# Attention with pooled queries and a gated MLP on one core: the remainder of each tile of p in two instructions, a planner that may prefer a form of product, and new ranks

## The chip, the cores and the metric

The kernel runs on one core of a Trainium2 chip. The metric is device time in microseconds (us) of one execution; the times are given as a median over repeated executions. The core has TensorE (PE, matrix products; PEld is its weight load), VectorE (DVE), ScalarE (ACT), GpSimd (POOL) and SyncE (SP, which here only issues transfers).

## The reference, cut to what matters

```python
def _attn_ref(q, k, v):                       # each (4, 8, 1152, 64), float32
    q_pool = q.reshape(B, H, S // 2, 2, D).mean(axis=3)
    scores = scale * np.matmul(q_pool, k.transpose(0, 1, 3, 2))
    scores = scores - np.max(scores, axis=-1, keepdims=True)
    attn = np.exp(scores)
    attn = attn / (np.sum(attn, axis=-1, keepdims=True) + 1e-09)
    return np.matmul(attn, v)

x = attn_out.transpose(0, 2, 1, 3).reshape(2304, 512)
h = x @ w_in                                  # w_in (512, 2048)
g = h * (1.0 / (1.0 + np.exp(-1.702 * h)))
return g @ w_out                              # w_out (2048, 512)
```

## The kernel before

**Attention.** The 32 heads are taken as 16 pairs. A pair has 9 tiles of scores, each 128 query rows by 1152 keys: 4 of head A, 4 of head B and one ("L") that holds the last 64 rows of both. That makes 144 tiles, numbered n. The 36 tiles of the first four pairs work in f32: scores (L629), transposes of p on TensorE (L751, evacuated at L256 or L258), and products with v (L774). The other 108 tiles split each f32 operand into an f16 head and an f16 remainder. For such a tile the steps are: S, six products (L658) into the single score buffer `s` of PSUM; M, the row maximum, which also copies the scores to the tile `p` (L672, DVE) and so frees `s`; B, a small addition to the maximum (L705); E, the exponential in place (L679, ACT); H (`p_hi`), the f16 head of p, written to one half of a tile `hl`; L (`p_lo`), the remainder p minus head, 1152 columns, written to the other half (L713, one instruction on DVE or POOL); T (`p_tr`), one DMA transpose of the whole `hl` (L726, queue of SP) into `pt` or `ptl`; then, once four tiles (or the L tile) are there, 54 products with v (L739). There are three `hl` buffers; H of a tile waits until the transpose that read the buffer three tiles back has landed.

**MLP.** Rows of x come in 9 blocks of 256. Each block has 8 steps j: 24 products h (L957), tanh (L965, ACT), gate (L971, DVE), `moe_hi` (g's f16 head, L256) and `moe_lo` (its remainder, L982, DVE), then 12 products o (L993). The f16 weights are made early in the kernel from the raw loads (L283 to L330). A block can start when all heads of its batch are done.

**The order.** Nothing is scheduled by hand. A planner (class `Plan`) holds every step as a task with an engine, a cost, a rank, predecessors and buffers. It simulates the engines and writes the order out; on the chip each engine runs its instructions in that order. At each step the planner takes, for each engine, the tasks that could start within `wait` of the earliest one, and of these the one of the lowest rank; the engine whose choice starts first goes next. A task with `or_on` may go to either of two engines, to whichever comes to it first. `movable` lists the kinds for which the second engine is allowed. Costs are multiplied by `slack` (for PE it is an added delay of each operand from another engine). The planner never lets a POOL task overlap a DVE task marked `two`. Tasks of TensorE carry a `mode`, the form of their product (0: the default, among them f16 scores of A and B, h, o and all transposes; 3: products with v, the rows of reciprocals, f16 scores of L; 4 and 5: f32 scores); a change of mode is charged `SWITCH`, 0.095 us. Ranks are n plus a constant of the kind; products h and o stand at 1,000,000 plus their sequence number, so attention always goes first and the MLP fills in.

`copy(e, ...)` issues an ACT activation (L256), a DVE copy (L258) or, with a scale, a DVE `tensor_scalar` (L260). `x_hi` and `x_even` write the f16 heads of x; `q_hi`, `k_hi`, `v_hi` and `w_hi` those of q, k, v and the weights.

Of the kernel before, what the change touches and what calls it, by code (L numbers as in the profile page):

```python
# [15 lines left out]
ALU = mybir.AluOpType  # L16
# [7 lines left out]
class Plan:  # L24
# [10 lines left out]
    DMA_IN, DMA_OUT, SWITCH = 0.8, 1.6, 0.095  # L35

    def __init__(self, sizes, wait, slack):
        self.sizes, self.wait, self.slack, self.tasks, self.users, self.takers = sizes, wait, slack, [], {}, {}

    def add(self, name, eng, cost, rank, fn, after=(), take=(), use=(), dma=0.0, or_on=None, two=False, mode=0, tr=False):  # L40
# [20 lines left out]
    def order(self):  # L61
        self.busy = {}
        left = {id(t): len(t["after"]) for t in self.tasks}
        ready = {(id(t), e): 0.0 for t in self.tasks for e in t["on"]}
        heirs = {}
        for t in self.tasks:
            for a in t["after"]:
                heirs.setdefault(a, []).append(t)
        pend = dict(self.users)
        ended = {}  # L70
        taken = {tag: [] for tag in self.sizes}
        free = {e: 0.0 for e in ("PE", "ACT", "DVE", "POOL", "SP")}
        queue = {e: [t for t in self.tasks if e in t["on"] and not left[id(t)]] for e in free}
        dma_free, lock, mode, out = 0.0, 0.0, 0, []

        def start(t, e):
            s = max(free[e], ready[id(t), e])
            if e == "POOL" or e == "DVE" and t["two"]:
                s = max(s, lock)
            more = {}  # L80
            for tag, _ in t["take"]:
                held = taken[tag]
                at = len(held) + more.get(tag, 0) - self.sizes[tag]
                more[tag] = more.get(tag, 0) + 1
                if at >= 0:
                    key = held[at]
                    if pend[key]:
                        return None
                    s = max(s, ended[key] + (self.slack["PE"] if e == "PE" else 0.0))
            return s  # L90

        while len(out) < len(self.tasks):
            best = None
            for e, q in queue.items():
                c = [(s, t) for s, t in ((start(t, e), t) for t in q) if s is not None]
                if not c:
                    continue
                s0 = min(s for s, _ in c) + self.wait.get(e, 0.0)
                s, t = min(((s, t) for s, t in c if s <= s0), key=lambda x: (x[1]["rank"], x[0]))
                if best is None or s < best[0]:  # L100
                    best = (s, t, e)
            assert best is not None, "the buffers taken are not given back"
            s, t, eng = best
            for e in t["on"]:
                queue[e].remove(t)
            cost = t["on"][eng]
            if eng != "PE":
                cost *= self.slack[eng]
            if eng == "PE":
                cost += self.SWITCH * (t["mode"] != mode)  # L110
                mode = t["mode"]
            end = free[eng] = self.run_pe(s, cost) if eng == "PE" else s + cost
            if eng == "POOL" or eng == "DVE" and t["two"]:
                lock = end
            if t["tr"]:
                free[eng] = dma_free = max(end, dma_free + t["dma"])
                end = dma_free + 2.05
            elif t["dma"]:
                dma_free = max(s + self.DMA_IN, dma_free) + t["dma"]
                end = dma_free + self.DMA_OUT  # L120
            out.append((t, eng))
            seen = end + self.HOP[eng]
            for tag, key in t["take"]:
                taken[tag].append(key)
            for key in t["use"]:
                pend[key] -= 1
                ended[key] = max(ended.get(key, 0.0), seen)
            for h in heirs.get(t["name"], ()):
                for e in h["on"]:
                    at = free[e] if e == eng and (e == "PE" or h["name"][0] == t["name"][0]) else seen + (self.slack["PE"] if e == "PE" else 0.0)  # L130
                    ready[id(h), e] = max(ready[id(h), e], at)
                left[id(h)] -= 1
                if not left[id(h)]:
                    for e in h["on"]:
                        queue[e].append(h)
        self.span = max(free.values())
        return out
# [3 lines left out]
def kernel(  # L141
# [27 lines left out]
    B, H, S, D = q.shape  # L169
# [14 lines left out]


    rank = dict(
        w1=1635.4577871165, w1_rate=0.1876384407, w2=1964.3304764093, w2_rate=0.0010521929,
        w1_cut=3141.8757239327, w1_cut_rate=51.5930924503, w2_cut=-186.6998375499, w2_cut_rate=1.8487508169,
        v_max=330.999166611, load=-550.3041412927, prep=894.9078087958, max=-1755.14139546,
        exp=-460.1572995655, p_hi=-10.305124868, p_lo=1244.8028802268, pv=1153.6831869514, x=1717.9360493586,  # L190
        recip=1660.8177940748, w_tr=1074.7852256343, w_ev=329.2480174456, g=-2009.7431374895,
        pv_b=-1699.9111894481, max_b=1557.6887587647, p_lo_b=594.8157896537, prep_b=-1564.592405644,
        v=1630.1595431886, lift=-579.2269003092,
    )
    movable = dict(DVE=('qk_ev', 'w_hi', 'k_hi', 'v_hi', 'x_even', 'w_sign'), POOL=('p_lo', 'denom'))
    wait = dict(PE=0.073718, ACT=0.133022, DVE=0.295657, POOL=0.285145)
    slack = dict(PE=0.297637, ACT=1.031989, DVE=1.023033, POOL=1.19561, SP=1.076504)
    sizes = dict(
        qraw=1, qs=1, kraw=1, kn=1, qn=1, kT=2, qT=2, vraw=2, vhl=1,
        p=3, hl=3, pt=3, ptl=1, xt=2, xf=2, raw=4, th=2, gf=2, g=3, osb=2, s=1, tr=1, pv=1, h=1, o0=1, o1=1,  # L200
    )
    plan = Plan(sizes, wait, slack)
# [32 lines left out]
    T = {}  # L235
# [6 lines left out]
    def on(kind, **cost):  # L242
        return {e: c for e, c in cost.items() if kind in movable[e]}
# [4 lines left out]
    def dve(n, psum=False, fast=False):  # L248
        return n / (1920 if fast else 960) + (0.065 if psum else 0.068)
# [91 lines left out]
    for i in range(32):  # L341
        c, kk = divmod(i, 4)
# [7 lines left out]
            or_on=on("w_exp", POOL=1.06),  # L350
# [10 lines left out]
            take=[("h", cs)] if first else []  # L361
# [8 lines left out]
    for c in range(8):  # L370
        for h in range(2):
            e = 2 * (c % 4) + h
            r = rank["w1_cut"] + e / rank["w1_cut_rate"] if c < 4 else rank["w2_cut"] + e / rank["w2_cut_rate"]
            after = [("w_scale", c // 4)] + [("w_mul", 4 * c + 2 * h + e) for e in range(2)]
            if c:
# [3 lines left out]
                or_on=on("w_hi", DVE=dve(1024, fast=True) + 0.06),  # L379
# [180 lines left out]
    for g in pairs:  # L560
# [7 lines left out]
        for i, (what, a) in enumerate((w, a) for w in "qkv" for a in range(2)):  # L568
            key = (what + "raw", G)
# [3 lines left out]
            if what == "k" and not G:  # L573
# [5 lines left out]
                use=[key] if a else [], dma=1.05,  # L579
# [3 lines left out]
        if g.wide:  # L583
            for i, (what, lo, hi) in enumerate(PARTS):
                pk = ("qkp", G, i)
                take = [(f"o{i % 2}", pk)] + ([("kT", kt)] if i == 0 else [("qT", qt)] if i == 1 else [])
# [121 lines left out]
        t = new("hl", ("hl", n), [128, 2, S], F16)  # L708
        copy(e, t[:, 0, :], T["p", n].rearrange("p c f -> p (c f)"))

    def p_lo(e, n):
        t = T["hl", n]
        (nc.vector if e == "DVE" else nc.gpsimd).tensor_tensor(  # L713
            out=t[:, 1, :], in0=T["p", n].rearrange("p c f -> p (c f)"), in1=t[:, 0, :], op=ALU.subtract
        )

    def p_tr(n):
# [115 lines left out]
    for n, (g, kind, t) in enumerate(tile_of):  # L833
# [25 lines left out]
        if g.whole:  # L859
            for c in range(3):  # L860
                pb = ("pb", n, c)
                plan.add(("X", n, c), "PE", 0.33, n + rank["w_tr"], lambda n=n, c=c: w_tr(n, c),
                         [("E", n)] + ([("X", n, c - 1)] if c else []),
                         take=[(f"o{(3 * n + c) % 2}", pb)], use=[("p", n)])
                plan.add(
                    ("Y", n, c), "ACT", act(384, True), n + rank["w_ev"], lambda e, n=n, c=c: w_ev(e, n, c),
                    [("X", n, c)] + ([("Y", n, 0)] if c else before), take=[] if c else take,
                    use=[pb] + ([key] if c else use), or_on=on("w_ev", DVE=dve(384, True)),
                )
        else:  # L870
            plan.add(("H", n), "ACT", act(1152, ptr=1), n + rank["p_hi"], lambda e, n=n: p_hi(e, n),
                     [("E", n)] + ([("H", n - 1)] if n and not tile_of[n - 1][0].whole else []),
                     use=[("p", n)], take=[("hl", ("hl", n))],
                     or_on=on("p_hi", DVE=dve(1152, fast=True) + 0.06), two=True)
            plan.add(("L", n), "DVE", dve(1152) + 0.06, n + rank["p_lo"] + (rank["p_lo_b"] if n >= 72 else 0.0),
                     lambda e, n=n: p_lo(e, n), [("H", n)], use=[("p", n), ("hl", n)], two=True,
                     or_on=on("p_lo", POOL=2.36))
            plan.add(
                ("T", n), "SP", 2.9, n - 1, lambda n=n: p_tr(n),
                [("L", n)] + before, take=take,  # L880
                use=use + [("hl", n)], dma=1.84, tr=True,
            )
        if kind == "A" or t % 2 == 0 and kind == "B":
# [255 lines left out]
```

## Time and profile before

| what | value |
|---|---|
| median of 3 runs | 800.97 us (798.48 to 801.73) |
| the profiled execution: its own time | 798.88 us |
| the profiled execution: span from first to last instruction | 797.1 us |
| PE busy in it | 767.6 us (96%) |
| ACT, DVE, POOL busy | 601.5 (75%), 564.4 (71%), 270.1 (34%) |

The profile shows one execution. "Busy" is the time in which an engine had at least one instruction; PE's ends are modelled because its products are pipelined. A wait names the instruction that came last before the waiting one could start.

### The profile page before, as it was taken

To read this page: it belongs to the slowest core of one execution; us is meant where nothing else is said; L and a number is where in the kernel's file an instruction comes from. 1 tells how busy PE (TensorE), PEld (TensorE's weight loads), DVE (VectorE), ACT (ScalarE), POOL (GpSimd) and SP (SyncE) were. 2 spreads that over 40 slices of the span, in tenths; PEclk is the share of its full clock that TensorE was granted. 3 is DMA by queue.
4 is the path that set the end of the run, shared out by engine and by line. 5 is a ranking of instruction groups with operands and counts; after the bars stand their busy time and mean duration, and the time that the engine had idled before them with its cause. 6 is when DMAs were issued, how large, how long until landed. Compare 5 with 4: busy or idle time off the path is not lost.

```text
span 797.1 us, 16744 instructions
## 1 busy us (share of the span) xinstructions
PE 767.6 (96%) x6756; PEld 514.8 (65%) x6756; DVE 564.4 (71%) x883; ACT 601.5 (75%) x1031; POOL 270.1 (34%) x164
## 2 busy tenths in 40 slices
PE   6999999999999999999999989999999999999998
PEld 3556565656566676666766666656666667766664
DVE  5867997689988869697787858688867785222222
ACT  5989988899888879697887879787987887232322
POOL 2232222145544442625235354521555423000000
PEclk9999999999999999999999999999999999999999
DMA  8644233459999999999999999999999979010000
GB/s 308 197 154 148 101 120 130 165 117 194 197 193 211 195 204 200 207 214 206 215 192 217 197 202 196 207 194 197 202 222 196 168 130 177 2 27 1 28 1 27
DMA packets 336143, 128.77 MB, mean 162 GB/s; under 512 B 311232, under 2 KB 321472, under 8 KB 336064
## 3 DMA queue, kind: packets, MB, share of 16 engines
q1 hardware_dynamic: 335776, 127.10, 76.7%
q8 instruction: 53, 0.87, 0.4%
q10 hardware_dynamic: 288, 0.59, 0.2%
q14 instruction: 26, 0.21, 0.1%
HBM read 45.09 MB, written 4.72 MB: 62 GB/s over the span
## 4 chain that ended last, share of the span: by engine, by line
PE 59%; DVE 13%; DMA 10%; ACT 7%; issue 6%; POOL 2%; SPq 2%; DVEq 0%; POOLq 0%; ACTq 0%
PE o L993 16%; PE h L957 15%; PE s L658 8%; PE pv L739 8%; DMA pt<-hl 5%; DVE p L672 4%; PE s L629 3%; PE pv L774 3%; PE o L751 3%; DMA ptl<-hl 3%; ACT p L679 2%; ACT hl L256 2%; DMA raw<-in_moe_w_in_dram 2%; PE tr L786 2%; DVE wbuf L330 1%
## 5 line engine op out<-in xcount | busy, mean ns | idle before, releaser
L713 POOL TENSOR_TENSOR hl<-p,hl 128x1152 f16<-128x1152 f32 x75 | 186.3, 2487 | 209.1 <-ACT hl L256 167.5
L672 DVE TENSOR_SCALAR_CACHE_REDUCE p<-s,e_s 128x1152 f32<-128x1152 f32 x144 | 203.5, 1413 | 52.7 <-PE s L658 31.1
L993 PE MATMUL o<-wbuf,g 128*128 128x512 f16 x864 | 206.2, 379 | 0.0
L957 PEld LDWEIGHTS <-wbuf 128*128 128x128 f16 x1728 | 168.0, 98 | 42.7 <-issue 6.8
L679 ACT ACTIVATE p<-p,nm 128x1152 f32<-128x1152 f32 x144 | 180.2, 1251 | 7.7 <-DVE p L672 4.3
L256 ACT ACTIVATE hl<-p 128x1152 f16<-128x1152 f32 x108 | 124.8, 1156 | 25.5 <-DMA pt<-hl 18.7
L993 PEld LDWEIGHTS <-g 128*128 128x128 f16 x864 | 83.0, 98 | 83.8 <-issue 2.3
L658 PE MATMUL s<-kT,qT 128*128 128x384 f16 (+1 forms) x720 | 123.9, 327 | 2.8 <-DVE p L672 2.7
L957 PE MATMUL h<-x16a,wbuf 128*128 128x256 f16 x960 | 118.0, 275 | 1.7 <-DVE gf L971 1.6
L971 DVE SCALAR_TENSOR_TENSOR gf<-th,h 128x512 f32<-128x512 f32 x72 | 49.2, 683 | 81.5 <-ACT th L965 81.3
L965 ACT ACTIVATE th<-h,t_s 128x512 f32<-128x512 f32 x72 | 49.0, 680 | 74.1 <-PE h L957 73.9
L957 PE MATMUL h<-wbuf 128*128 128x256 f16 x768 | 90.9, 273 | 0.7 <-DVE gf L971 0.7
L658 PEld LDWEIGHTS <-qT 128*128 128x128 f16 (+1 forms) x720 | 62.2, 100 | 45.0 <-issue 9.9
L739 PEld LDWEIGHTS <-vhl 128*64 128x64 f16 x1944 | 80.6, 111 | 15.9 <-issue 8.5
L739 PE MATMUL pv<-pt,vhl 128*64 128x256 f16 x1296 | 76.1, 273 | 2.4 <-DMA pt<-hl 2.4
L982 DVE SCALAR_TENSOR_TENSOR g<-gf,g 128x512 f16<-128x512 f32 x72 | 59.0, 819 | 17.3 <-ACT g L256 17.1
L307 POOL TENSOR_TENSOR wbuf<-raw 128x512 f32<-128x512 f32 x32 | 33.7, 1060 | 82.0 <-ACT raw L303 66.8
L256 ACT ACTIVATE g<-gf 128x512 f16<-128x512 f32 x72 | 44.7, 621 | 18.5 <-DVE gf L971 18.5
L713 DVE TENSOR_TENSOR hl<-p,hl 128x1152 f16<-128x1152 f32 x33 | 45.7, 1386 | 12.2 <-ACT hl L256 11.7
L751 PE MATMUL o<-idf,p 128*128 128x128 f32 x324 | 50.1, 284 | 3.5 <-ACT pt L256 2.9
L629 PE MATMUL s<-kT,qT 64*128 64x512 f32 (+3 forms) x240 | 49.5, 524 | 1.5 <-DVE p L672 1.5
L751 PEld LDWEIGHTS o<-idf,p 128*128 128x128 f32 x324 | 35.4, 141 | 19.4 <-ACT pt L256 8.9
(101 smaller groups left out, 790.5 us busy)
## 6 DMA issues: line engine op xcount, KB each, us to landing
vraw<-in_v_dram SPq DMA_DIRECT2D x32, 288.0 KB, 3.5
kraw<-in_k_dram SPq DMA_DIRECT2D x30, 288.0 KB, 4.1
qraw<-in_q_dram SPq DMA_DIRECT2D x32, 256.0 KB, 3.8
raw<-in_moe_w_in_dram SPq DMA_DIRECT2D x16, 512.0 KB, 5.3
raw<-in_moe_w_out_dram SPq DMA_DIRECT2D x16, 512.0 KB, 5.7
out_dram<-osb SPq DMA_DIRECT2D x16, 256.0 KB, 3.0
pt<-hl SPq DMA_TRANSPOSE x96, 5.2
qraw<-in_q_dram SPq DMA_DIRECT2D x32, 32.0 KB, 3.4
```

The costliest lines, as they stand in the source:

```text
L256: nc.scalar.activation(out=out, in_=in_, func=ACTF.Copy, scale=1.0 if scale is None else scale)
L629: nc.tensor.matmul(out=ps[m, bank, 0:128 * (last - first)], lhsT=qT[h, (j - half) % NJ, m], rhs=kT[h, first:last].rearrange("p j c -> p (j ...
L658: nc.tensor.matmul(out=ps[m, c, 0:384], lhsT=st, rhs=T["kT", g.P][:, o:o + 3].rearrange("p r c -> p (r c)"), start=(l == 0), stop=(l == 1),)
L672: nc.vector.tensor_scalar(out=p, in0=s, scalar1=e_s[:, g.P:g.P + 1], scalar2=None, op0=ALU.mult, op1=ALU.min, accum_out=m)
L679: nc.scalar.activation(out=p, in_=p, func=ACTF.Exp, bias=T["nm", n], scale=-1.0, accum_out=sm)
L713: (nc.vector if e == "DVE" else nc.gpsimd).tensor_tensor(out=t[:, 1, :], in0=T["p", n].rearrange("p c f -> p (c f)"), in1=t[:, 0, :], op=A ...
L739: nc.tensor.matmul(out=ps[64 * a:64 * (a + 1), 0:w], lhsT=T["vhl", g.P][:, a, g.block[a][c], m], rhs=pt[:, l * KR + c, o:o + w], start=(pa ...
L751: nc.tensor.transpose(ps[:, 128 * i:128 * (i + 1)], T["p", n][:, c, 128 * i:128 * (i + 1)], idf)
L957: nc.tensor.matmul(out=h[:, e, :], lhsT=w1(2 * j + e, l, kk), rhs=x_rhs(blk, m, kk), start=(kk == 0 and l == 0 and m == 0), stop=(kk == KD ...
L971: nc.vector.scalar_tensor_tensor(out=gf, in0=T["th", blk, j], scalar=1.0, in1=T["h", blk, j].rearrange("p e n -> p (e n)"), op0=ALU.add, o ...
L982: nc.vector.scalar_tensor_tensor(out=g[:, 1].rearrange("p e n -> p (e n)"), in0=T["gf", blk, j], scalar=2.0 ** -16, in1=g[:, 0].rearrange( ...
L993: nc.tensor.matmul(out=o, lhsT=g[:, l, e, 128 * t:128 * (t + 1)], rhs=w2(fc, m), start=(fc == 0 and l == 0 and m == 0), stop=(fc == KFF - ...
```

## The change

`p_lo` becomes two tasks per tile, each of 576 columns, each free to go to DVE or POOL; the transpose waits for both. The planner's choice subtracts `stay` (7.04) from the rank of a PE task whose mode is that of the task before it. `movable` for DVE loses `k_hi`, `v_hi`, `x_even` and gains `x_hi`, `q_hi`, `moe_hi`, `p_hi`. All ranks, the `wait` windows and the `slack` factors are new.

```diff
-                s, t = min(((s, t) for s, t in c if s <= s0), key=lambda x: (x[1]["rank"], x[0]))
+                s, t = min(((s, t) for s, t in c if s <= s0), key=lambda x: (x[1]["rank"] - self.stay * (e == "PE" and x[1]["mode"] == mode), x[0]))
...
-        exp=-460.1572995655, p_hi=-10.305124868, p_lo=1244.8028802268, pv=1153.6831869514, x=1717.9360493586,
-        recip=1660.8177940748, w_tr=1074.7852256343, w_ev=329.2480174456, g=-2009.7431374895,
-        pv_b=-1699.9111894481, max_b=1557.6887587647, p_lo_b=594.8157896537, prep_b=-1564.592405644,
...
+        exp=-689.1559533665, p_hi=-215.4333082359, p_lo=1595.0361505333, pv=1170.2986869698,
+        x=2179.8268281408, recip=1650.9699594071, w_tr=1053.0065825932, w_ev=98.4213600032,
+        g=-2195.4805088551, pv_b=-1953.8227656797, max_b=1410.7413160855, p_lo_b=57.4810218892,
...
-    movable = dict(DVE=('qk_ev', 'w_hi', 'k_hi', 'v_hi', 'x_even', 'w_sign'), POOL=('p_lo', 'denom'))
-    wait = dict(PE=0.073718, ACT=0.133022, DVE=0.295657, POOL=0.285145)
-    slack = dict(PE=0.297637, ACT=1.031989, DVE=1.023033, POOL=1.19561, SP=1.076504)
+    movable = dict(DVE=('x_hi', 'w_hi', 'qk_ev', 'q_hi', 'moe_hi', 'p_hi', 'w_sign'), POOL=('p_lo', 'denom'))
+    wait = dict(PE=0.02865, ACT=0.112216, DVE=0.177087, POOL=0.959385)
+    slack = dict(PE=0.107219, ACT=1.026002, DVE=1.033503, POOL=1.055202, SP=1.040576, stay=7.040544)
...
-    def p_lo(e, n):
-        t = T["hl", n]
+    def p_lo(e, n, half):
+        t, c = T["hl", n], slice(half * S // 2, (half + 1) * S // 2)
         (nc.vector if e == "DVE" else nc.gpsimd).tensor_tensor(
-            out=t[:, 1, :], in0=T["p", n].rearrange("p c f -> p (c f)"), in1=t[:, 0, :], op=ALU.subtract
+            out=t[:, 1, c], in0=T["p", n].rearrange("p c f -> p (c f)")[:, c], in1=t[:, 0, c], op=ALU.subtract
         )
...
-            plan.add(("L", n), "DVE", dve(1152) + 0.06, n + rank["p_lo"] + (rank["p_lo_b"] if n >= 72 else 0.0),
-                     lambda e, n=n: p_lo(e, n), [("H", n)], use=[("p", n), ("hl", n)], two=True,
-                     or_on=on("p_lo", POOL=2.36))
+            for half in range(2):
+                plan.add(("L", n, half), "DVE", dve(576) + 0.06,
+                         n + rank["p_lo"] + (rank["p_lo_b"] if n >= 72 else 0.0),
+                         lambda e, n=n, half=half: p_lo(e, n, half), [("H", n)], use=[("p", n), ("hl", n)], two=True,
+                         or_on=on("p_lo", POOL=1.2))
             plan.add(
                 ("T", n), "SP", 2.9, n - 1, lambda n=n: p_tr(n),
-                [("L", n)] + before, take=take,
+                [("L", n, 0), ("L", n, 1)] + before, take=take,
```

## Rows read from the trace of the kernel before

**Rows 1.** The page: busy time by engine, and PE by 40 slices.
```profile
PE 767.6 (96%) x6756; PEld 514.8 (65%) x6756; DVE 564.4 (71%) x883; ACT 601.5 (75%) x1031; POOL 270.1 (34%) x164
...
PE   6999999999999999999999989999999999999998
```

**Rows 2.** Two stretches: length, busy us of PE, PEld, DVE, ACT, POOL; clock, DMA.
```profile
180.00:650.00 470.00, 456.53 (x4483) 316.21 (x4478) 378.36 (x569) 391.52 (x638) 207.17 (x104) 1.00 1.05 198
650.00:798.00 148.00, 143.50 (x1095) 96.41 (x1092) 47.09 (x68) 54.15 (x87) 11.02 (x6) 1.00 0.23 45
```

**Rows 3.** Waits of PE, 150 to 650 us: total us, times, longest.
```profile
PE s L658 <- DVE p L672: 2.7, 5, 0.9
PE pv L739 <- DMA pt<-hl: 2.4, 3, 1.4
PE h L957 <- DVE gf L971: 2.4, 2, 1.6
PE tr L786 <- DVE w_r L697: 1.7, 2, 0.9
PE pv L739 <- DVE tr L266: 1.6, 1, 1.6
PE o L751 <- ACT pt L256: 1.5, 1, 1.5
PE pv L739 <- DMA ptl<-hl: 1.3, 1, 1.3
PE tr L447 <- DVE qkv L435: 1.0, 1, 1.0
```

**Rows 4.** The chain that ended last, from 420 us: start, us, what.
```profile
423.97 2.19 POOL hl L713
426.16 6.71 DMA ptl<-hl
```

**Rows 5.** Instructions by line: count, shortest/median/longest in ns, first and last start.
```profile
L713 POOL TENSOR_TENSOR hl<-p,hl x75: 2368/2377/3311, 177.6 to 663.1; 128x1152 f16<-128x1152 f32 x75
...
L713 DVE TENSOR_TENSOR hl<-p,hl x33: 1328/1359/2364, 174.2 to 669.6; 128x1152 f16<-128x1152 f32 x33
...
L420 POOL TENSOR_TENSOR qs<-qraw x15: 1405/1413/2472, 18.5 to 582.6; 128x576 f32<-128x576 f32 x15
...
L260 DVE TENSOR_SCALAR kn<-kraw,s_qkv x4: 812/884/1551, 157.2 to 478.4; 128x1152 f16<-128x1152 f32 x4
L260 DVE TENSOR_SCALAR vhl<-vraw,s_qkv x3: 804/811/816, 441.8 to 644.7; 128x1152 f16<-128x1152 f32 x3
```

**Rows 6.** Groups by line and shape: count, busy us, mean ns, idle before.
```profile
L420 DVE TENSOR_TENSOR qs<-qraw 128x576 f32<-128x576 f32 x1 | 0.8, 759 | 5.7 <-DMA qraw<-in_q_dram 5.7
```

**Rows 7.** Timeline of DVE and of POOL, 411 to 414 us: start, us.
```profile
411.49 2.36 DVE L713 TENSOR_TENSOR hl<-p,hl 128x1152 f16<-128x1152 f32 x1
413.77 0.68 DVE L982 SCALAR_TENSOR_TENSOR g<-gf,g 128x512 f16<-128x512 f32 x1
...
411.22 1.41 POOL L420 TENSOR_TENSOR qs<-qraw 128x576 f32<-128x576 f32 x1 [8.10 <-DMA qraw<-in_q_dram]
```

**Rows 8.** Groups by line and shape, 180 to 650 us.
```profile
L256 ACT ACTIVATE hl<-p 128x1152 f16<-128x1152 f32 x100 | 115.5, 1156 | 25.5 <-DMA pt<-hl 18.7 <-DMA ptl<-hl 6.0
...
L982 DVE SCALAR_TENSOR_TENSOR g<-gf,g 128x512 f16<-128x512 f32 x47 | 41.1, 874 | 1.3 <-ACT g L256 1.1
L256 ACT ACTIVATE g<-gf 128x512 f16<-128x512 f32 x47 | 29.0, 618 | 3.4 <-DVE gf L971 3.4
...
L256 ACT ACTIVATE kn<-kraw,s_qkv 128x1152 f16<-128x1152 f32 x8 | 9.9, 1240 | 0.0
```

**Rows 9.** Waits of ACT and of DVE, 180 to 650 us: total us, times, longest.
```profile
ACT hl L256 <- DMA pt<-hl: 18.7, 14, 2.9
...
ACT hl L256 <- DMA ptl<-hl: 6.0, 4, 3.3
...
DVE p L672 <- PE s L658: 27.0, 33, 2.1
```

More of the change, by code (lines that the diff above doesn't have):

```diff
@@ L37, in __init__ @@
     def __init__(self, sizes, wait, slack):
+        self.stay = slack["stay"]
         self.sizes, self.wait, self.slack, self.tasks, self.users, self.takers = sizes, wait, slack, [], {}, {}
@@ L186 @@
     rank = dict(
-        w1=1635.4577871165, w1_rate=0.1876384407, w2=1964.3304764093, w2_rate=0.0010521929,
-        w1_cut=3141.8757239327, w1_cut_rate=51.5930924503, w2_cut=-186.6998375499, w2_cut_rate=1.8487508169,
-        v_max=330.999166611, load=-550.3041412927, prep=894.9078087958, max=-1755.14139546,
-        exp=-460.1572995655, p_hi=-10.305124868, p_lo=1244.8028802268, pv=1153.6831869514, x=1717.9360493586,
-        recip=1660.8177940748, w_tr=1074.7852256343, w_ev=329.2480174456, g=-2009.7431374895,
-        pv_b=-1699.9111894481, max_b=1557.6887587647, p_lo_b=594.8157896537, prep_b=-1564.592405644,
-        v=1630.1595431886, lift=-579.2269003092,
-    )
-    movable = dict(DVE=('qk_ev', 'w_hi', 'k_hi', 'v_hi', 'x_even', 'w_sign'), POOL=('p_lo', 'denom'))
-    wait = dict(PE=0.073718, ACT=0.133022, DVE=0.295657, POOL=0.285145)
-    slack = dict(PE=0.297637, ACT=1.031989, DVE=1.023033, POOL=1.19561, SP=1.076504)
+        w1=1526.5067291696, w1_rate=1.3300764709, w2=1923.6545876625, w2_rate=0.0513201332,
+        w1_cut=3217.4085614408, w1_cut_rate=2.1003628513, w2_cut=-251.8402408958, w2_cut_rate=26.5596121916,
+        v_max=371.6022042096, load=-662.7022384162, prep=1066.4435968055, max=-1665.2681370577,
+        exp=-689.1559533665, p_hi=-215.4333082359, p_lo=1595.0361505333, pv=1170.2986869698,
+        x=2179.8268281408, recip=1650.9699594071, w_tr=1053.0065825932, w_ev=98.4213600032,
+        g=-2195.4805088551, pv_b=-1953.8227656797, max_b=1410.7413160855, p_lo_b=57.4810218892,
+        prep_b=-1371.0731187368, v=1655.390877664, lift=-532.5087172742,
+    )
+    movable = dict(DVE=('x_hi', 'w_hi', 'qk_ev', 'q_hi', 'moe_hi', 'p_hi', 'w_sign'), POOL=('p_lo', 'denom'))
+    wait = dict(PE=0.02865, ACT=0.112216, DVE=0.177087, POOL=0.959385)
+    slack = dict(PE=0.107219, ACT=1.026002, DVE=1.033503, POOL=1.055202, SP=1.040576, stay=7.040544)
     sizes = dict(
```

## The prediction, made before the changed kernel was run

> **What bounds the kernel now.** I read the busy times first, then stretches of the span, then PE's waits, then the chain. PE is busy 767.6 of 797.1 us, and the slices show it at nine tenths or more except in the first, in one in the middle and in the last [rows 1]. The change removes, adds and shortens no product, so what it can reach is PE's idle time, 797.1 - 767.6 = 29.5 us, and whatever small gaps the modelled ends of products hide. I split the 29.5 us with two stretches [rows 2]. From 180 us, where the MLP's products begin to fill PE, to 650 us PE is idle 470.0 - 456.5 = 13.5 us. From 650 to the end it is idle 147.1 - 143.5 = 3.6 us, which is about the last evacuation and store; nothing here touches that. The first 180 us hold the remaining 12.4 us, of which the first slice (20 us at six tenths) has some 8, before the first loads and the first transposes. So about 17 us (13.5 and some 4 early) can be won, 2% of the span, and anything beyond that would have to come from shorter switches of form.
>
> PE's waits from 150 to 650 us say who causes the idle time there [rows 3]. Products with v that wait for a transposed tile have 2.4 + 1.3 us, and I add the 1.6 us that stand against a DVE scalar step, since that is also a product with v whose operand is a transpose: 5.3 us in 5 waits. Everything else (scores behind the row maximum 2.7, h behind the gate 2.4, the reciprocals' rows 1.7, transposes of p 1.5, the maxima 1.0) is 9.3 us in 11 waits. The chain that ended last runs through such a product: the remainder on POOL from 423.97, then a transpose from issue to landing of 6.71 us, with PE waiting for it [rows 4]. The remainder is thus on the path in a few places only.
>
> **Part 1, the remainder in halves.** On POOL one takes 2.377 us, on DVE 1.359 us [rows 5]. For 576 columns no row shows the same instruction. On POOL the bounds are half of 2.377, 1.19 us, and the f32 sum of the same width, 1.413 us [rows 5]; I take 1.28 us, near their middle. On DVE the same width took 0.759 us [rows 6], and half of 1.359 is 0.68; I take 0.76. Two on POOL then cost 2.56 us (0.18 more than now), two on DVE 1.52 us (0.16 more), and one on each 1.28 us if they run together. Whether they do is the question. A DVE remainder that started at 411.49, 0.27 us into a POOL sum, took 2.36 us in place of 1.359; POOL's sum ended at 412.63 and DVE's instruction 1.22 us after that [rows 7]. So DVE did next to nothing while POOL worked, and I take the halves one behind the other: 0.76 + 1.28 = 2.04 us, 0.34 us less than now. At the 5 waits for transposes that is 1.7 us. The lower bound is all 5.3 us (halves together, 1.1 us earlier at each of 5), the upper one 5 x 0.18 = 0.9 us lost.
>
> The Trainium skill (SBUF — State Buffer, section "Who interferes with whom") says that a DVE instruction with two SBUF inputs and a GpSimd instruction that reads SBUF exclude each other, the second blocking until the first is done. The trace agrees with it in the row of 2.36 us. By the rule the pair of halves gains the 1.7 us taken above, without it up to 5.3 us.
>
> The longer instructions themselves cost nothing in the sum: 0.18 us times about 100 tiles is 18 us of POOL, which is busy 207 of 470 us, and 0.16 us for each tile on DVE, which is busy 378 of 470 [rows 2]; if that cover were gone, the 18 us would come onto the transposes' chain. The transpose now waits for two engines, but still starts with the later one. There is a second effect. While POOL holds a tile, DVE's two-input instructions stretch: the remainder of g takes 0.68 us alone [rows 7] and 0.874 on the mean [rows 8], 47 x 0.19 = 9 us of DVE time in the stage. A block by a half lasts at most 1.28 us in place of 2.38, so about half of this, 4 us of DVE time, comes back, and the step stands between gate and o.
>
> **Part 2, other engines.** The heads of p (1.156 us) and g (0.618 us) on ACT [rows 8] may now go to DVE. The nearest rows for p are the heads of k and v on DVE at the same width and types, 0.804 to 1.551 us with medians of 0.884 and 0.811 [rows 5]; I take 0.85. For g, 512 of 1152 columns, the bounds are 0.38 (in proportion to 0.85) and 0.618 (no faster than ACT); I take 0.48. If a third goes, ACT sheds 33 x 1.156 + 16 x 0.618 = 48 us of 391 and DVE gains 33 x 0.85 + 16 x 0.48 = 36 us of 378. In return heads of k and v (seven, 1.24 us each on ACT [rows 8]) and of x go back to ACT, some 10 us. `q_hi` and `x_hi` have the same answer as p's heads and are few. ACT, now at 83% of the stage, and DVE, at 80%, change places. This can shorten the waits behind ACT and lengthen those behind DVE.
>
> **Part 3, `stay`.** It is worth 7 units of rank, so it decides only between PE tasks of different modes whose ranks lie within 7. From tile 36 on the scores stand at n (36 to 143), products with v and reciprocals' rows at n - 784, the pair's maxima at n - 325, h and o at a million. In the first 36 tiles scores stand at n, transposes of p at n + 1053, products with v at n + 1170, weights' sums at 1527 to 1538 and from 1924 up. No two of different modes come within 7. I cost this edit at nothing, not by cover but because it decides nothing; the bound is the same.
>
> **Part 4, ranks, windows and slack.** The order of kinds on PE and DVE in the long stage stays as it was (x, g, preparation, row maximum, then the remainder). PE's operands are assumed ready 0.107 in place of 0.298 us after the producer, so products are ordered closer behind their operands: fewer planned gaps, more short real waits. I can't price this by a row. I put parts 2 and 4 and the shorter blocks of part 1 together: of the 9.3 us of other waits some 4 go. The bounds are all 9.3 us and the few early us gained (13 in all), and 13 lost (the rival below, with as much again of early waits as stand there now).
>
> **Sum.** -1.7 - 4 = -5.7 us, about -6. The profiled execution took 798.88 us, 1.8 more than its span, and so would take 793; the median of the runs stands 2.1 us above it, so the forecast against the median is 800.97 - 6 = 795 us.
>
> **Rivals.**
>
> *PE bound, nothing reached.* The waits move elsewhere, since PE is at 97% of the stage and fills with the MLP [rows 2]; each of the 16 waits is under 1.6 us [rows 3] and a new order makes others. For it speaks that all engines but PE have slack; against it that 5.3 us hang on the very instruction that is cut. It gives 797 to 805, at the middle 801.
>
> *DVE gets ACT's waits (slower).* p's head waits for an `hl` buffer, 18.7 + 6.0 us in 18 waits, up to 3.3 us [rows 9]. On ACT this holds up exponentials. On DVE it holds up the row maximum queued behind it, that the single score buffer, that the next scores, and behind those, in order, the MLP's products. A third of 24.7 us is 8 us, so 809. It decides once a DVE wait exceeds the 27.0 / 33 = 0.8 us for which DVE itself now waits for scores [rows 9]; the mean wait for a buffer, 24.7 / 18 = 1.4 us, does. Against it: with less on ACT and the remainder sooner the transposes start sooner, and the planner counts the buffers.
>
> *Nearly all of the idle time goes.* 801 - 17 = 784, if the waits of the long stage vanish. For it: no single cause is large. Against it: 16 waits with seven causes don't vanish together.
>
> **How the numbers follow.** A measurement tells about 0.5% from no change, here 4 us: 797 to 805. Chances: forecast 0.47 (788 to 797 its own range), nothing reached 0.29, DVE waits 0.18 (805 to 814), nearly all idle gone 0.06 (below 788). So faster 0.53, same 0.29, slower 0.18. The range goes from 784 to 808, which leaves out about 2 in 10, most of it above.
>
> **What would show it.** Right: 216 remainders of 576 columns, near 1.28 us on POOL and 0.76 on DVE; PE idle about 23 us; products with v waiting for transposes below 4 us; heads of p and g on DVE near 0.85 and 0.48; the number of changes of form on PE as before. Wrong: scores waiting for the row maximum well above 2.7 us; DVE waiting for transposes in front of p's head; POOL halves above 1.4 us. The forecast fails if PE's busy time itself changes by more than a few us, which I hold to be fixed, or if the early stage is reordered so that the MLP begins later.

## The result and the profile after

The changed kernel takes 811.95 us (median of 4 runs, 808.2 to 812.9), the kernel before on the same chip 799.73 us: a ratio of 1.0142, 95% interval 1.0099 to 1.0185. It is slower by 12 us, where 6 us faster was forecast. The profiled execution took 811.16 us with a span of 809.4 us, 12.3 us longer than that of before.

First the page of the changed kernel, which answers to [rows 1]: busy time by engine, and PE by slices.

```profile
PE 772.5 (95%) x6756; PEld 516.4 (64%) x6756; DVE 581.1 (72%) x947; ACT 594.7 (73%) x999; POOL 299.0 (37%) x240
...
PE   6999999989899999989898999999999999999998
```

PE idles 809.4 - 772.5 = 36.9 us in place of 29.5, and its busy time, which I held to be fixed, grew by 4.9 us though it runs the same 6756 products. Small waits that the modelled ends of products hide may be the reason; no view shows it. The sum is the 12.3 us.

Now stretches of the changed kernel (columns as in [rows 2]), and one of the kernel before.

```profile
180.00:650.00 470.00, 447.90 (x4403) 309.51 (x4403) 383.46 (x612) 380.26 (x607) 231.93 (x175) 1.00 1.06 197
325.00:500.00 175.00, 163.36 (x1588) 112.37 (x1589) 137.87 (x218) 136.51 (x220) 80.58 (x62) 1.00 1.06 200
500.00:650.00 150.00, 146.05 (x1484) 101.70 (x1482) 118.37 (x197) 123.14 (x199) 73.20 (x56) 1.00 1.07 196
```

```profile
325.00:500.00 175.00, 170.43 (x1686) 118.11 (x1686) 138.39 (x206) 144.18 (x237) 75.62 (x38) 1.00 1.08 205
```

From 180 to 650 us PE idles 22.1 us, 8.6 more than in [rows 2], and 7.1 of these lie between 325 and 500 us, where PE also gets through 98 products fewer (1588 against 1686). The time is lost in the long stage, before the MLP is alone.

The waits of PE in the changed kernel, 150 to 650 us, which answer to [rows 3]:

```profile
PE pv L740 <- DMA pt<-hl: 5.1, 8, 1.6
PE tr L787 <- DVE w_r L698: 4.1, 6, 1.8
PE s L659 <- DVE p L673: 3.7, 6, 1.6
PE pv L740 <- DMA ptl<-hl: 3.4, 4, 1.4
PE tr L793 <- DVE w_r L698: 2.5, 4, 1.6
PE h L960 <- DVE gf L974: 1.6, 2, 1.2
PE o L752 <- ACT pt L257: 1.5, 3, 1.1
PE pv L740 <- DVE s_qkv L273: 0.6, 1, 0.6
PE tr L448 <- DVE qkv L436: 0.5, 1, 0.5
PE s L659 <- DMA kT<-kn: 0.5, 1, 0.5
```

Products with v now wait 8.5 us for transposes, in 12 waits; I had 5.3 in 5, and expected below 4. The rows of reciprocals wait 6.6 us, against 1.9. All rows but those two of the transposes come to 15.0 us, where I had 9.3 and expected some 4 less. Of the changed instructions themselves the line view, which answers to [rows 5], and the groups by shape, which answer to [rows 8], show:

```profile
L714 POOL TENSOR_TENSOR hl<-p,hl x151: 1268/1283/2400, 180.6 to 666.2; 128x576 f16<-128x576 f32 x151
...
L714 DVE TENSOR_TENSOR hl<-p,hl x65: 743/758/1833, 175.2 to 674.4; 128x576 f16<-128x576 f32 x65
```

```profile
L714 POOL TENSOR_TENSOR hl<-p,hl 128x576 f16<-128x576 f32 x151 | 213.9, 1434 | 166.0 <-ACT hl L257 106.0 <-issue 46.0 <-DVE o_s L947 6.3
...
L257 ACT ACTIVATE hl<-p 128x1152 f16<-128x1152 f32 x106 | 122.6, 1157 | 51.4 <-DMA pt<-hl 32.3 <-DMA ptl<-hl 17.7 <-ACT nm L706 0.6
...
L985 DVE SCALAR_TENSOR_TENSOR g<-gf,g 128x512 f16<-128x512 f32 x72 | 52.3, 726 | 16.7 <-ACT g L257 15.7
...
L257 ACT ACTIVATE g<-gf 128x512 f16<-128x512 f32 x48 | 29.9, 624 | 20.7 <-DVE gf L974 20.4
...
L261 DVE TENSOR_SCALAR g<-gf 128x512 f16<-128x512 f32 x24 | 12.9, 536 | 0.8
...
L259 DVE CAST hl<-p 128x1152 f16<-128x1152 f32 x2 | 1.5, 752 | 0.0
```

The halves cost what was forecast (medians of 1.283 and 0.758 us), 151 of them on POOL. A third of g's heads went to DVE (24 of 72), but only two of p's heads. So the heads of p still wait on ACT for an `hl` buffer, 50 us now where [rows 9] have 24.7: the transposes that give the buffers back land later, relative to the work that fills them.

### The profile page after: what moved, and what is told of

It is laid out like the page before. It is cut to its first block, busy times and chain, and to the rows that moved or that the text cites. A ratio compares the mean times of both kernels' runs of the same rounds, so it can differ in the third digit from the quotient of the medians.

```text
span 809.4 us, 16977 instructions
## 1 busy us (share of the span) xinstructions
PE 772.5 (95%) x6756; PEld 516.4 (64%) x6756; DVE 581.1 (72%) x947; ACT 594.7 (73%) x999; POOL 299.0 (37%) x240
## 4 chain that ended last, share of the span: by engine, by line
PE 53%; DMA 17%; DVE 11%; ACT 7%; issue 5%; POOL 3%; SPq 2%; POOLq 0%; DVEq 0%; ACTq 0%
PE h L960 13%; PE o L996 12%; DMA pt<-hl 9%; PE s L630 5%; PE o L752 5%; PE s L659 4%; PE pv L775 4%; PE pv L740 4%; DMA ptl<-hl 4%; DVE p L673 3%; ACT hl L257 3%; POOL hl L714 3%; ACT p L680 2%; PE h L313 2%; DMA qraw<-in_q_dram 1%
## 5 line engine op out<-in xcount | busy, mean ns | idle before, releaser
L714 POOL TENSOR_TENSOR hl<-p,hl 128x576 f16<-128x576 f32 x151 | 213.9, 1434 | 166.0 <-ACT hl L257 106.0
L257 ACT ACTIVATE hl<-p 128x1152 f16<-128x1152 f32 x106 | 122.6, 1157 | 51.4 <-DMA pt<-hl 32.3
L960 PE MATMUL h<-x16a,wbuf 128*128 128x256 f16 x960 | 115.7, 273 | 1.3 <-DVE gf L974 1.2
L740 PEld LDWEIGHTS <-vhl 128*64 128x64 f16 x1944 | 81.0, 111 | 23.2 <-issue 12.3
L659 PEld LDWEIGHTS <-qT 128*128 128x128 f16 (+1 forms) x720 | 65.1, 100 | 45.8 <-issue 11.0
L740 PE MATMUL pv<-pt,vhl 128*64 128x256 f16 x1296 | 78.3, 274 | 5.3 <-DMA pt<-hl 5.1
L714 DVE TENSOR_TENSOR hl<-p,hl 128x576 f16<-128x576 f32 x65 | 59.6, 934 | 14.5 <-ACT hl L257 14.1
L985 DVE SCALAR_TENSOR_TENSOR g<-gf,g 128x512 f16<-128x512 f32 x72 | 52.3, 726 | 16.7 <-ACT g L257 15.7
L421 POOL TENSOR_TENSOR qs<-qraw 128x576 f32<-128x576 f32 x15 | 22.9, 1529 | 71.0 <-DMA qraw<-in_q_dram 55.7
```

The lines of the kernel that those rows point to most:

```text
L257: nc.scalar.activation(out=out, in_=in_, func=ACTF.Copy, scale=1.0 if scale is None else scale)
L659: nc.tensor.matmul(out=ps[m, c, 0:384], lhsT=st, rhs=T["kT", g.P][:, o:o + 3].rearrange("p r c -> p (r c)"), start=(l == 0), stop=(l == 1),)
L714: (nc.vector if e == "DVE" else nc.gpsimd).tensor_tensor(out=t[:, 1, c], in0=T["p", n].rearrange("p c f -> p (c f)")[:, c], in1=t[:, 0, c] ...
L740: nc.tensor.matmul(out=ps[64 * a:64 * (a + 1), 0:w], lhsT=T["vhl", g.P][:, a, g.block[a][c], m], rhs=pt[:, l * KR + c, o:o + w], start=(pa ...
L960: nc.tensor.matmul(out=h[:, e, :], lhsT=w1(2 * j + e, l, kk), rhs=x_rhs(blk, m, kk), start=(kk == 0 and l == 0 and m == 0), stop=(kk == KD ...
L985: nc.vector.scalar_tensor_tensor(out=g[:, 1].rearrange("p e n -> p (e n)"), in0=T["gf", blk, j], scalar=2.0 ** -16, in1=g[:, 0].rearrange( ...
```

## The experiments

Each comparison is with the kernel before on the same chip. e9 to e14 and e18 leave out part of the work: they show where time goes, and are no faster kernels.

| run | what is changed | us | ratio to before, interval |
|---|---|---|---|
| e1 | before, same order, remainder in halves | 798.6 | 0.998 (0.996 to 1.000) |
| e5 | after, same order, remainder whole | 815.7 | 1.020 (1.018 to 1.023) |
| e2 | before with halves, planned anew | 816.4 | 1.020 (1.016 to 1.023) |
| e3 | after with whole remainder, planned anew | 836.1 | 1.045 (1.041 to 1.049) |
| e4 | after with old wait and slack, planned anew | 823.1 | 1.029 (1.025 to 1.033) |
| e6, e7 | before, planned anew with one number moved by 0.8 and 0.2% | 811.4, 820.2 | 1.016 (1.011 to 1.020), 1.026 (1.024 to 1.028) |
| e8 | after, planned anew with one number moved by 2.6% | 822.7 | 1.029 (1.026 to 1.032) |
| e9, e13 | before, same order, only heads, only remainders of p transposed | 789.8, 790.0 | 0.988 (0.985 to 0.991), 0.987 (0.985 to 0.990) |
| e10, e14 | after, same order, only heads, only remainders of p transposed | 788.2, 788.0 | 0.986 (0.983 to 0.990), 0.985 (0.983 to 0.987) |
| e18 | e7, same order, only heads of p transposed | 804.2 | 1.006 (1.004 to 1.009) |
| e11, e12 | e8 and e7 with blocks 2 to 5 of the MLP on a constant, planned anew | 818.2, 805.4 | 1.022 (1.018 to 1.027), 1.008 (1.005 to 1.010) |
| e15 | after, same order, two transposes per tile | 803.4 | 1.004 (1.002 to 1.006) |
| e17 | before, same order, two transposes per tile | 793.1 | 0.992 (0.989 to 0.994) |
| e16 | before, same order, halves and two transposes per tile | 790.2 | 0.988 (0.985 to 0.990) |

**The halves by themselves.** Since the planner rewrites the whole order whenever a task changes, I first kept an order and changed the instruction alone. In e1 the planner sees one task as before, and the function issues it in two pieces:

```diff
     def p_lo(e, n):
         t = T["hl", n]
-        (nc.vector if e == "DVE" else nc.gpsimd).tensor_tensor(
-            out=t[:, 1, :], ...
+        for half in range(2):
+            c = slice(half * S // 2, (half + 1) * S // 2)
+            (nc.vector if e == "DVE" else nc.gpsimd).tensor_tensor(
+                out=t[:, 1, c], in0=T["p", n].rearrange("p c f -> p (c f)")[:, c], in1=t[:, 0, c], op=ALU.subtract
+            )
```

> The kernel before with its own order kept, each remainder issued as two instructions of 576 columns one behind the other on the engine that had the whole (75 tiles on GpSimd, 33 on VectorE). Theory H (the halves themselves make the transposed tiles late): 0.18 us more per tile on GpSimd plus more collisions with VectorE; slower by 4 to 9 us against before, products with v waiting for transposes 8 us and more. Theory S (the small delay allowance and waits of the new planner put products too close behind their operands) and theory R (the new order as a whole, no single part): no change, within 2 us of before.

798.57 us, 2.0 us less than before, at the edge of what can be told from nothing. Theory H falls here. The counterpart e5 keeps the order of the changed kernel and puts the remainder back into one instruction:

```diff
     def p_lo(e, n, half):
-        t, c = T["hl", n], slice(half * S // 2, (half + 1) * S // 2)
+        if n not in first_half:
+            first_half.add(n)
+            return
+        t, c = T["hl", n], slice(0, S)
```

> The changed kernel with its own order kept; the first half of each remainder is left out and the second, at its own place and on its own engine, does all 1152 columns in one instruction. Theory H (the halves are the loss): 800 to 804. Theory R (the order as a whole is the loss, and halves in it are worth little): 809 to 815, within 4 us of the changed kernel.

815.68 us, 3.7 us above the changed kernel (1.020 against 1.014 of the kernel before, with intervals that touch). So in either order the halves cost nothing; they may be worth 2 to 4 us, which neither run tells from nothing. The loss is in the order.

**Which part of the change made the order worse?** Three runs undo or do one part, each planned anew. e2 takes the two tasks of the diff into the kernel before, with its numbers:

> The kernel before with the remainder as two tasks, freely placed and planned anew; ranks, waits, slack and movable kinds as before. H: 807 to 813, the loss of the change is here. S: within 3 us of before. R: anywhere from 3 to 12 us slower, since the order is new.

e3 takes the single task back into the changed kernel:

> The changed kernel with the remainder as one task again (costs of the kernel before), all else as changed, planned anew. H: back to 799 to 803. S: stays at 809 to 815. R: anywhere from 803 to 815, and not as fast as before.

e4 takes the old `wait` and `slack` into it:

```diff
-    wait = dict(PE=0.02865, ACT=0.112216, DVE=0.177087, POOL=0.959385)
-    slack = dict(PE=0.107219, ACT=1.026002, DVE=1.033503, POOL=1.055202, SP=1.040576, stay=7.040544)
+    wait = dict(PE=0.073718, ACT=0.133022, DVE=0.295657, POOL=0.285145)
+    slack = dict(PE=0.297637, ACT=1.031989, DVE=1.023033, POOL=1.19561, SP=1.076504, stay=7.040544)
```

> The changed kernel with the wait windows and slack factors of the kernel before (PE 0.298 in place of 0.107 us of delay, GpSimd factor 1.196 in place of 1.055), planned anew. S: 799 to 804. H: stays at 809 to 815. R: anywhere from 803 to 815.

816.4, 836.1 and 823.1 us: no part undone brings the time back, two of them make it much worse. All three lie outside the ranges of all three theories, R's too, which had at most 12 us of loss in e2 and 815 us in e3 and e4. In these orders a lower clock adds to the loss: the mean granted clock is 0.989, 0.984 and 0.985 in e2, e3 and e4, against 0.998 in the kernel before and in the changed one. In e3 it is 0.50, its lower level, from 510.4 to 527.5 us, after PE had idled 2.3 of the 10.4 us ahead of that. Three controls then move one number of the planner that no instruction sees:

```diff
-    slack = dict(PE=0.297637, ACT=1.031989, DVE=1.023033, ...      # e6: PE=0.3; e7: DVE=1.025
...
-    slack = dict(PE=0.107219, ...                                  # e8: PE=0.11
```

> The kernel before, planned anew with one number moved by less than one per cent that no instruction sees (the delay allowance of TensorE 0.300 in place of 0.2976 us). R: a new order loses as the changed one does, 806 to 830. H and S (small delay allowance): no part of the change is in it, so 798 to 803.

> The same with another number (the factor on VectorE's costs 1.025 in place of 1.023). R: 806 to 830, and not the same time as the other replanned one. H and S: 798 to 803.

> The changed kernel with its delay allowance of TensorE 0.110 in place of 0.107 us, so another order by the same ranks. R: 806 to 835, more likely above the changed kernel than below. H and S: as the changed kernel, 809 to 815.

811.4 and 820.2 us from the kernel before without any part of the change, 822.7 from the changed one. With the changed kernel that makes seven other orders, 1.4 to 4.5% slower than the one of the kernel before. The ranges of theory R, made wider for these three, hold: a new order can cost as much as the whole change, whichever number brought it about.

It does not follow that the changed kernel loses for the same reason as these. The planner's own simulated length of an order (its `span`, which no chip run is part of) is 777.8 us for the kernel before and 786.1 and 794.2 for e6 and e7: of the 12 and 21 us that they lose on the chip, 8 and 16 stand in the plan already. For the changed kernel the plan has 770.0 us, 8 less than for the kernel before, and the chip takes 12 more. If the changed kernel's order is kept and timed by the same simulation with the old `slack`, it comes to 791.1 us, 13 above the kernel before; the old factor of PE, POOL or SP alone gives 782.8, 783.0 or 777.7. By this estimate the order is short only under the smaller allowances, which is theory S. It is an estimate by the planner's costs, and no run shows it. e4 does not exclude it, because e4 is yet another order, planned at 806.0 us.

With `stay` at 0 the planner of the changed kernel writes the same order as with 7.04 on every engine, so that edit does nothing.

**What does a new order lose?** I looked at the one queue that I had not read before predicting. The timeline of SP's queue in the kernel before:

```profile
347.09 10.16 SPq L726 DMA_TRANSPOSE pt<-hl  x3
357.35 2.69 SPq L512 DMA_TRANSPOSE qT<-qn  x1
360.13 2.74 SPq L508 DMA_TRANSPOSE kT<-kn  x1
362.93 0.57 SPq L409 DMA_DIRECT2D qraw<-in_q_dram  x1
363.55 0.48 SPq L413 DMA_DIRECT2D qraw<-in_q_dram  x1
364.13 3.04 SPq L726 DMA_TRANSPOSE pt<-hl  x1
367.21 0.59 SPq L409 DMA_DIRECT2D qraw<-in_q_dram  x1
```

There is hardly a gap of 0.1 us. All such rows from 325 to 500 us, laid end to end, fill 168 of 175 us in the kernel before (96%), and 165 in the changed one (94%). They hold no wait for a remainder: in both kernels none of the 108 rows of p's transposes begins before its remainder has ended. The Trainium skill (Perfetto Trace Analysis, section 'What "DMA-bound" means') names an issuing engine's track that is solid DMA slices as a bound of its own, and these rows come within 4 to 6% of it. A pair of heads has 11 transposes, and by the median of 3.2 us these alone are 35 us of the some 42 us from one pair's last product with v to the next pair's. So attention has a pace of its own, and PE is not the only full resource. e9 and e10 take that load off, in the same orders:

```diff
-        src = T["hl", n].rearrange("p l f -> p (l f)")
+        src = T["hl", n][:, 0, :]                          # e13, e14: [:, 1, :]
...
-        nc.sync.dma_start_transpose(out=d, in_=src)
+        nc.sync.dma_start_transpose(out=d[:, 0:KR], in_=src)
...
-    TERMS = [(0, 0), (0, 1), (1, 0)]
+    TERMS = [(0, 0), (0, 1), (0, 0)]
```

> The kernel before, its order kept, with only the f16 heads of p transposed (half of each transpose; the third group of products with v reads the heads again in place of the remainders, so TensorE does the same work, and the remainders of p are left out of the result). Theory Q (the queue of transposes paces attention, and TensorE loses what the queue loses): 785 to 793, products with v no longer wait. Theory W (waits of TensorE on VectorE in a fixed order): 794 to 799.

> The changed kernel, its order kept, with the same cut. Q: 788 to 797, within 5 us of the kernel before with the cut, so that most of the 12 us goes with the transposes. W: 803 to 810, the distance of 10 us and more stays.

789.8 and 788.2 us: the whole difference is gone. The views by line and by stretch, e9 first, then e10:

```profile
L726 SPq DMA_TRANSPOSE pt<-hl x96: 1242/1304/2403, 173.3 to 661.1; - x96
```

```profile
325.00:500.00 175.00, 174.92 (x1719) 120.69 (x1718) 151.43 (x238) 150.16 (x242) 90.19 (x69) 1.00 0.76 150
```

A transpose of half the tile holds the queue for 1.30 us, not 1.6, and in the changed kernel's order PE now idles 0.1 us from 325 to 500 us where it idled 11.6. With PE so full, the cut shows that the loss needs the long transposes, not that it has no other condition. The cut also halves what the transposes move: the share of the DMA engines falls from 1.06 to 0.76 here. Whether the queue itself or the engines behind it set the length of its rows, these runs don't separate. In e9 and e10 a transpose of heads also needs no remainder. e13 and e14 separate that: they transpose the remainders alone, as short, but each behind its remainder.

> The kernel before, its order kept, with only the f16 remainders of p transposed (half of each transpose, but each waits for its remainder; the third group of products with v reads the first half again, the heads of p are left out of the result). Theory QL (the length of the transposes in their queue): within 3 us of the run in which only heads were transposed, 787 to 793. Theory QW (the transposes are late because the remainders are): 794 to 799.

> The changed kernel, its order kept, with the same cut. QL: 785 to 792, the distance to the kernel before stays gone. QW: 798 to 808, since here the queue waited 94 us for remainders on GpSimd against 41 before.

790.0 and 788.0 us, the same as with heads. QL's ranges hold and QW's fail: the length of the transposes in a full queue turns this order's irregularities into waits of PE. With transposes this short it does not matter that each waits for its remainder; whether it matters while the queue is full, the two runs don't show. The 94 and 41 us in the expectation of e14 are no idle time of the queue: that view also counts semaphores which arrive inside a row. From 180 to 650 us the queue stood empty until a remainder ended for some 11 us in the changed kernel and 14 in the kernel before.

**Does that hold for the other orders?** e18 is e7's order with the cut of e9:

> The replanned kernel before (factor 1.025, 820.2 us), its order kept, with only the heads of p transposed. QL: the loss of the new order goes with the queue, 787 to 797. If the queue accounts for the changed kernel alone and other new orders lose by themselves: 805 to 815.

804.2 us, between the two ranges. The cut takes 16 us off e7, but in e9 it takes 9 off the kernel before as well: of the 21 us between those two orders 14 stay, and only 7 go with the transposes. What e10 and e14 show for the changed kernel does not hold for this order. Stretches in e7 and then e18:

```profile
490.00:520.00 30.00, 24.57 (x189) 15.73 (x188) 24.11 (x35) 22.94 (x38) 7.66 (x4) 0.94 0.95 175
```

```profile
490.00:520.00 30.00, 24.30 (x234) 17.66 (x233) 21.95 (x31) 27.65 (x47) 14.42 (x8) 0.94 0.83 169
```

Here PE idles 5.4 and 5.7 us of 30 with or without the cut, and the granted clock is 0.94 on the mean in both. It is the end of a batch: there is no product h from 494.5 to 518.3 us in e7 and from 484.5 to 508.1 us in e18, the 32 steps of four blocks being done while the next batch's attention is not. So this order has a second loss, the MLP out of work. In e11 and e12 blocks 2 to 5 need no x:

```diff
+        if 2 <= blk <= 5:
+            return x_c                       # a constant tile
         return x16[b % 2][:, l, kk, 256 * u:256 * (u + 1)]
...
-        xs = [("last_lo",)] if b == B else ...
+        xs = [] if 2 <= blk <= 5 else [("last_lo",)] if b == B else ...
```

> The replanned changed kernel (822.7 us) with blocks 2 to 5 of the MLP reading a constant tile in place of x, so that TensorE has MLP work before a batch's attention is done (those blocks' outputs are left out), planned anew. Theory D (around the ends of batches the MLP runs dry and TensorE goes at attention's pace): 796 to 806. Q and W without D: 812 to 830.

> The same cut in the kernel before replanned with the factor 1.025 (820.2 us). D: 796 to 806. Without D: 810 to 828.

818.2 and 805.4 us. The second fits theory D (15 of the 21 us), the first misses it and hardly moves (4 us). As the planner wrote yet another order for each, the two don't settle how much the MLP's lack of work costs.

**A version that beats both.** If a half holds the queue for 1.30 us, two cost 2.6 in place of 3.2. e15 and e16 give each tile two transposes, in the order of the changed kernel and in that of e1:

```diff
-        nc.sync.dma_start_transpose(out=d, in_=src)
+        for l in range(2):
+            nc.sync.dma_start_transpose(out=d[:, KR * l:KR * (l + 1)], in_=T["hl", n][:, l, :])
```

> The changed kernel, complete, its order kept, with each transpose of a tile of p as two (heads, then remainders). A half took 1.30 us on the queue where nothing else was, a whole 3.2. QL: if two halves take 2.6 to 3.0 us, 795 to 806; if they take as long as a whole, 808 to 816. QW: the heads go early and only half of the work is behind the remainder, 800 to 806.

> The kernel before with its order, remainders in two instructions on the same engine (798.6 us) and each transpose of a tile of p as two. QL: 788 to 796 if two halves take 2.6 to 3.0 us, else 796 to 802. QW: 794 to 798.

> The kernel before with its order and whole remainders, each transpose of a tile of p as two (heads, then remainders). If the two transposes alone bring the gain of the run with both, 789 to 793; if the halves of the remainder bring their part of it, 793 to 797.

e15 takes 803.4 us, 8.6 us less than the changed kernel, and lies in the ranges of QL and QW alike; e16 takes 790.2, complete and 1.2% faster than before, in QL's range alone; e17, without the halves, 793.1, on the border of its two ranges. The line and the stretch of e16:

```profile
L728 SPq DMA_TRANSPOSE pt<-hl x192: 1247/1342/3493, 174.0 to 666.2; - x192
```

```profile
325.00:500.00 175.00, 173.62 (x1709) 120.17 (x1707) 142.35 (x221) 146.54 (x240) 80.75 (x63) 1.00 1.13 208
```

By the medians two transposes cost 2 x 1.342 = 2.7 us, half a microsecond less than one. By the sum less is won: all rows of p's transposes take 324 us in e16 and e17 in place of 339, which is 0.14 us a tile, since some halves hold the queue for up to 3.5 us. PE idles 1.4 us in the stretch in which the kernel before idles 4.6 and the changed one 11.6. There is a second possible source of the gain: the transpose of the heads need not wait for the remainder. In e17 32 of the 108 start before it has ended, and the queue stands empty until a remainder ends for 5 us from 180 to 650 us in place of 14. The runs don't tell the two apart. The halves' share, 793.1 to 790.2, agrees with e1 in size, though the two intervals overlap.

## Why the prediction was wrong

**The step that failed** is in parts 2 and 4, summed as "of the 9.3 us of other waits some 4 go". A new order was treated as if it kept the old order's waits and took some away. In its place e5, which has the new order without the halves, measured 17 us more than the kernel before. PE's other waits rose from 9.3 to 15.0 us, and those for transposes, with the halves, from 5.3 to 8.5. Six other new orders cost 12 to 36 us, two of them of the kernel before with a number moved by under 1%. Part 4 had the direction itself, "fewer planned gaps, more short real waits", but counted the first and not the second. By the planner's simulation with the old `slack`, the new order would have come out 13 us long: an estimate, which could have been had beforehand. My upper bound for it, 13 lost, came from a different mechanism and was given too little weight.

**Behind it lies a reading that was missing.** I wrote that PE fills with the MLP, and that all engines but PE have slack. I read PE, ACT, DVE and POOL, but not the queue of SP, although [rows 2] show the DMA share at 1.05 and [rows 9] show ACT waiting for transposes. The queue was 96% full in the middle of the stage. With two full resources that feed each other, there is little slack to take up a new order's mistakes. For the changed kernel e10 and e14 bear this out; in e7's order the transposes account for about a third of the loss only.

**Point by point.**
- PE's idle time bounds the gain: nothing contradicts it, and e9, e14 and e16 win 9 to 12 us within the 17. That PE's busy time is fixed was wrong by 4.9 us.
- The halves: durations 1.28 and 0.76 us forecast, 1.283 and 0.758 measured. Their means are 1.434 and 0.934, with single ones up to 2.400 and 1.833, which fits blocking as in [rows 7]. Their gain, -1.7 us, was measured as -2.0 (e1, interval -3.4 to +0.2) and -3.7 (e5, intervals that touch). The size fits, but neither run tells it from nothing. That the gain comes through earlier transposes is not shown: in e13 and e14 it matters little when the remainder ends, but there the queue is not full.
- Shorter blocks of DVE: g's remainder went from 0.819 to 0.726 us on the mean over all 72, as argued (the line's mean in the page of each kernel).
- Other engines: a third of g's heads moved (0.536 us, 0.48 forecast). Of p's heads 2 of 108 moved, where I took a third (0.752 us, 0.85 forecast).
- `stay` decides nothing: right.
- The rival in which DVE takes over ACT's waits gave 809 us, but it is not what happened: with two of p's heads on DVE the scores' wait for the row maximum went from 2.7 to 3.7 us only. The number was near by chance. In the rival "nothing reached" I had written that a new order makes other waits, but not that it makes more.

What stays open: which rank or allowance makes the changed kernel's order put PE's work where the queue can't follow. The planner's simulation points to the smaller allowances of `slack`; e4 can't decide it, since it is a new order too. Ranks and movable kinds were not tried apart, because with each new order scattering by 10 us or more a single run could not tell.

## What to carry to other kernels

Where a planner writes the order, a change of any of its inputs is a new order, and its price can be bounded by replanning with a number that no instruction sees: here two such orders cost 1.6 and 2.6%, more than the whole change. Look first at the planner's own length of each order, and at the length that it gives the new order under the old allowances: a plan that is short only because its allowances were cut is no gain. To price an edit, keep the order and change the instruction alone; to price an order, keep the instructions. Before calling a kernel bound by one engine, lay the rows of each issuing queue end to end too: here a queue at 96% stood beside an engine at 97%, and e17, which changes the transposes alone, won 0.8%.

## What was not expected of the hardware

A DMA transpose of 128 x 1152 f16 holds the issuing queue for 1.30 us (median of 96 in e9, where a tile has this one alone) where one of 128 x 2304 holds it for 3.2. The shortest of each are 1.24 and 2.38 us, in proportion; the long ones are dearer in the full queue. Of those with no gap before them in the kernel before, the median is 2.7 us behind another transpose and 3.3 us behind a load. Two short ones in place of one long one, 1.34 us each by the median and 1.50 by the mean with all the work in place, gave 0.8% by themselves (e17), though not only the length of the rows may have done it.
